# A streamed-weight segment recurrence on one core: other granules stream, and their left passes move along

## The chip, the cores and the metric

The kernel runs on one core of one Trainium2 chip. The metric is the device time of one execution in microseconds. The engines are TensorE (PE, with its weight loads PEld), VectorE (DVE), ScalarE (ACT), GpSimd (POOL) and SyncE (SP), which here does nothing but issue transfers; 16 DMA engines move the data.

## What is computed

The output is the sum of three terms over `x` of 2048 x 1024 in bf16. The first is `x` itself. The second is an attention over 64 segments of 32 rows, in which each segment is preceded by 8 rows of memory, and the first 8 output rows of a segment are the memory of the next one. The third is an expert layer on the two rows with the highest router score. Cut to what matters:

```python
for s in range(n_seg):                      # 64 segments, one after the other
    h = concatenate([mem, xs], axis=1)      # 8 + 32 rows of 1024
    q, k, v = h @ Wq, h @ Wk, h @ Wv        # 32 heads of 128
    p = softmax(mask(q @ k.T * scale))
    o = (p @ v) @ Wo                        # 40 x 4096 @ 4096 x 1024
    mem = o[:, :M, :]                       # goes into the next segment
    outs.append(o[:, M:, :])
...
return x + A(xn) + B(xn)                    # xn: x with its rows normalised
```

The segments form a chain through `mem`, so all four weight matrices (8 MB each in bf16) are used again in each of 64 steps.

## The kernel before

The weights are cut into 64 **granules** of 128 partitions x 2048 columns, 512 KB each. Granules 0 to 47 are six phases of eight: q0, k0, q1, k1, v0, v1 (`PHASES`: matrix and half of the heads); granules 48 to 63 are the output projection. On-chip memory holds 44 of them for the whole run (`resident`, tiles `wres`). The other 20, listed in `STREAMED`, are loaded again in each segment, through a ring of `N_SLOT` = 5 tiles `g` of the pool `wstream`. In segment 0 they come from the inputs; copies of them are made meanwhile in a scratch tensor `wsc`, from which all later segments read. Granule 6 is streamed only in segment 0, since afterwards it stays in PSUM (`KEPT_WHOLE`); of granule 25 half stays there (`KEPT_PART`). So a later segment streams 18 whole granules and a half.

A segment runs through its granules in the order of their numbers. At each it does the **main** matmuls: four of 512 columns into `PSm` for granules 0 to 47 (L817), eight of 256 columns into `WO` for 48 to 63 (`project`, L586). At fixed places (`hook`) the attention work of the segment is put between them. Transfers are issued on SP in program order: when a streamed granule is done with, `release` calls `after`, and that calls `fetch`, which issues the next transfer of the endless list `flow` at L366. This issue waits for the slot's last reader on TensorE, which is the use of the granule five places earlier in the list.

Of a segment's 32 rows, 24 go through the main matmuls beside the 8 memory rows. The other 8 (the **left** rows) do not depend on the memory. They are gathered over four segments (a group) and go through the weights once per group, ahead of their use. That is a **left pass**: four matmuls of 512 columns per granule, into `PSl` (`left_pass`, L579) or `WL` (`project_left`, L598). The table `PASSES` says where each one runs: for a unit (q0, k0, q1, k1, v0, v1, o) and a place (segment of the group, phase, position) the granules whose left pass runs there. Phase 6 is the output projection, places 7 and 8 are the seam between two segments: 7 stands behind the add at L885 (`X <- WO, X`) that makes the new memory, 8 behind the turn of that memory into `ST`, the next segment's operand. A granule that is resident can have its pass anywhere; a streamed one has it where it is used anyway, or is held in its slot until then (`held`). `COPIES` says where a finished unit is copied out of PSUM.

In segment 0, SP issues the loads of residents, of `x` (tiles `XP`) and of the first streamed granules in one list, interleaved by granule number; the tiles `XP`, `MISC` and `XR` lie in the homes of the last residents, which are loaded when the statistics of the rows and the router scores (L254, L256) are done with them. In the last segment each resident's home that comes free takes a granule of the expert weights (`fetch_moe`).

Of the kernel before, what the change touches and what calls it, by code (L numbers as in the profile page):

```python
# [22 lines left out]

PHASES = [(0, 0), (1, 0), (0, 1), (1, 1), (2, 0), (2, 1)]

STREAMED = [2, 5, 6, 9, 13, 17, 21, 25, 29, 33, 36, 39, 42, 45, 47, 50, 53, 56, 59, 62]

UNIT_PHASE = {"q0": 0, "k0": 1, "q1": 2, "k1": 3, "v0": 4, "v1": 5, "o": 6}
PASSES = {
# [11 lines left out]
}  # L44

COPIES = {"q0": (1, 1, 0, "scalar"), "q1": (1, 5, 7, "vector"), "k0": (2, 2, 0, "scalar"), "k1": (2, 5, 7, "vector"),
# [4 lines left out]
def kernel(  # L51
# [44 lines left out]

    streamed = STREAMED
    assert len(streamed) == NG - N_RES
# [915 lines left out]
```

## Time and profile before

| | |
|---|---|
| median of 3 runs | 1866.62 us (1864.03 to 1872.82) |
| profiled execution | 1871.21 us |
| its span | 1869.1 us |
| instructions | 80529 |
| mean granted TensorE clock | 0.957 |
| bytes moved | 712.27 MB, mean 381 GB/s |

A row of the views names line, engine, operation and `out<-in` by the program's tiles. In the waits, "a <- b: t, n, m" says that a stood idle t us in all, n times and at most m us at once, until b. A row of the windows is start:end and length in us, then busy us (and instructions) of TensorE, its weight loads, VectorE, ScalarE and GpSimd, then the granted TensorE clock, the share of the 16 DMA engines' time and GB/s. That share can be a little over 1 since the records of packets overlap. In the order of time a row starts with its start and length in us and merges equal instructions (x8); what stands in brackets is the idle time ahead of it and what ended it.

### The profile page before, as it was taken

The numbers are of one execution on the slowest core, as the hardware profiler recorded it, in microseconds if no ns is written. First come the engines' busy times: TensorE is split into PE (matmuls) and PEld (weight loads), VectorE is DVE, ScalarE is ACT, GpSimd is POOL, SyncE is SP. The second block draws the span as 40 slices with busy tenths as digits, with TensorE's granted clock in tenths as the row PEclk, the third lists the DMA queues.
The fourth block names the chain that finished last, engine by engine and source line by source line (L and its number), as shares of the span: only waits on it lengthen the run. The fifth ranks groups of instructions, "written<-read, shape, count | busy, mean of one in ns | idle before, by whom it ended". The sixth has DMA issues, their size and how long they took to land.

```text
span 1869.1 us, 80529 instructions
## 1 busy us (share of the span) xinstructions
PE 1568.8 (84%) x34978; PEld 847.9 (45%) x34978; DVE 896.9 (48%) x2950; ACT 683.6 (37%) x1933; POOL 457.1 (24%) x898
## 2 busy tenths in 40 slices
PE   3458998898998988888899988988889988988764
PEld 1124444444444444444444444444445544444433
DVE  6725544554455444544554455544544455445430
ACT  1113433444343433434344334434334343433320
POOL 3111322213231322223132322323132221312220
PEclk8669999999999999999999999999999999999995
DMA  9999999999999999999999999999999999999998
GB/s 370 406 355 373 388 386 380 393 382 387 394 385 392 366 383 391 359 380 385 388 375 388 389 384 387 373 396 374 378 369 396 394 382 383 378 377 352 384 402 338
DMA packets 230322, 712.27 MB, mean 381 GB/s; under 512 B 39040, under 2 KB 52912, under 8 KB 229968
## 3 DMA queue, kind: packets, MB, share of 16 engines
q1 hardware_dynamic: 192592, 671.18, 93.0%
q0 software_dynamic: 28736, 28.08, 4.7%
q10 hardware_dynamic: 8640, 7.87, 1.2%
q8 instruction: 274, 4.49, 0.9%
q14 instruction: 80, 0.66, 0.1%
HBM read 694.32 MB, written 22.29 MB: 383 GB/s over the span
## 4 chain that ended last, share of the span: by engine, by line
DMA 61%; PE 32%; DVE 4%; issue 1%; ACT 1%; SPq 0%; ACTq 0%; DVEq 0%
DMA g<-wsc 54%; PE PSm L817 17%; PE WO L586 4%; PE PSl L579 4%; PE BT L649 2%; DMA XP<-in_A_x_dram 2%; PE WL L598 1%; DMA MW<-in_B_w_gate_dram 1%; DVE XR L256 1%; DMA MW<-in_B_w_up_dram 1%; DMA g<-in_A_Wq_dram 1%; DMA wres<-in_A_Wo_dram 1%; DMA g<-in_A_Wo_dram 1%; DMA MW<-in_B_w_down_dram 1%; DMA g<-in_B_w_down_dram 1%
## 5 line engine op out<-in xcount | busy, mean ns | idle before, releaser
L817 PE MATMUL PSm<-wres,ST 128*32 128x512 bf16 x8448 | 700.5, 383 | 6.5 <-DMA wres<-in_A_Wv_dram 3.5
L817 PEld LDWEIGHTS <-ST 128*32 128x32 bf16 x12288 | 323.6, 96 | 412.7 <-issue 168.2
L817 PE MATMUL PSm<-g,ST 128*32 128x512 bf16 x3588 | 360.0, 386 | 97.7 <-DMA g<-wsc 76.3
L586 PEld LDWEIGHTS <-OT 128*32 128x32 bf16 x8192 | 217.6, 97 | 166.6 <-issue 141.0
L836 ACT CAST XB<-PSm 128x512 bf16<-128x512 f32 x256 | 150.7, 589 | 283.9 <-PE PSm L817 280.8
L586 PE MATMUL WO<-wres,OT 128*32 128x256 bf16 x5632 | 237.6, 278 | 12.3 <-DMA wres<-in_A_Wo_dram 8.0
L495 POOL DMA_DIRECT2D LX<-ql_d x63 | 35.4, 562 | 814.0 <-PE WO L586 423.2
L586 PE MATMUL WO<-g,OT 128*32 128x256 bf16 x2560 | 133.3, 281 | 84.1 <-DMA g<-wsc 72.6
L579 PE MATMUL PSl<-wres,STL 128*32 128x512 bf16 x2112 | 184.5, 390 | 0.4 <-issue 0.4
L887 POOL DMA_DIRECT2D out_dram<-X x256 | 130.2, 515 | 211.9 <-DVE X L885 169.4
L664 DVE COPY KT<-BT 128x512 bf16<-128x512 bf16 x112 | 45.9, 410 | 278.7 <-issue 121.8
L281 POOL DMA_DIRECT2D X<-in_A_x_dram x256 | 130.1, 515 | 179.6 <-PE PSm L817 88.8
L389 ACT COPY BK<-KEPT 128x512 bf16<-128x512 bf16 x126 | 74.3, 590 | 131.2 <-PE WO L586 99.8
L657 ACT COPY QT<-BT 128x512 bf16<-128x512 bf16 x128 | 75.0, 586 | 127.1 <-PE BT L502 78.1
L649 PEld LDWEIGHTS <-XB 128*128 128x128 bf16 x1024 | 58.6, 98 | 117.1 <-ACT XB L836 75.2
L885 DVE TENSOR_TENSOR X<-WO,X 128x256 bf16<-128x256 f32 x64 | 27.2, 425 | 172.3 <-PE WO L586 172.3
L649 PE MATMUL BT<-IDENT,XB 128*128 128x128 bf16 x1024 | 102.2, 223 | 8.2 <-ACT XB L836 6.7
L579 PEld LDWEIGHTS <-STL 128*32 128x32 bf16 x3072 | 84.0, 98 | 53.0 <-issue 8.5
L846 ACT CAST VM<-PSm 128x512 bf16<-128x512 f32 x128 | 76.5, 598 | 83.3 <-PE PSm L817 82.8
L736 PEld LDWEIGHTS <-VM 32*128 32x128 bf16 x2048 | 65.1, 91 | 83.7 <-issue 72.7
L393 DVE COPY g<-KEPT 128x512 bf16<-128x512 bf16 x126 | 47.6, 420 | 101.7 <-PE PSm L817 51.5
L681 DVE TENSOR_TENSOR BS<-BS,CT 128x96 f32<-128x96 f32 (+1 forms) x256 | 59.1, 231 | 72.8 <-PE BS L674 68.3
(175 smaller groups left out, 2371.9 us busy)
## 6 DMA issues: line engine op xcount, KB each, us to landing
g<-wsc SPq DMA_DIRECT2D x1134, 512.0 KB, 6.0
g<-wsc SPq DMA_DIRECT2D x63, 256.0 KB, 5.7
LX<-ql_d POOLq DMA_DIRECT2D x63, 128.0 KB, 5.6
ql_d<-XBl ACTq DMA_DIRECT2D x60, 128.0 KB, 5.8
MW<-in_B_w_gate_dram SPq DMA_DIRECT2D x16, 448.0 KB, 9.5
MW<-in_B_w_up_dram SPq DMA_DIRECT2D x16, 448.0 KB, 9.1
wres<-in_A_Wk_dram SPq DMA_DIRECT2D x12, 512.0 KB, 11.9
MW<-in_B_w_down_dram SPq DMA_DIRECT2D x12, 512.0 KB, 10.1
```

What stands on the lines that cost most here:

```text
L281: nc.gpsimd.dma_start(out=X[s % 2][32 * g:32 * g + XM, :], in_=x2[s * SEG:s * SEG + XM, 256 * g:256 * (g + 1)])
L389: copy(out=back[c][:, :], in_=KEPT_COLS[KEPT_WHOLE][c])
L579: nc.tensor.matmul(PSl[32 * jq:32 * jq + 32, :], lhsT=STL[:, g % KC, :], rhs=part(Gv, jq), start=first_, stop=last_, tile_position=(0, 32 ...
L586: nc.tensor.matmul(PS[32 * g:32 * g + 32, 0:256], lhsT=lhs(h), rhs=Gv[:, D * hs + 256 * g:D * hs + 256 * (g + 1)], start=(first and hs == ...
L649: nc.tensor.transpose(out=PTq[:, il, :, :].rearrange("p j r -> p (j r)"), in_=XB[:, il * P:(il + 1) * P], identity=IDENT[:, :])
L657: nc.scalar.copy(out=QT[half][:, :, :], in_=pv)
L681: nc.vector.tensor_tensor(out=S4, in0=S4, in1=m, op=ALU.add)
L736: nc.tensor.matmul(o, lhsT=VM[half][q0:q0 + 32, il * P:(il + 1) * P], rhs=PTm[q0:q0 + 32, il, 0:NK], start=True, stop=False, tile_position ...
L817: nc.tensor.matmul(PSm[32 * jq:32 * jq + 32, :], lhsT=ST[:, kc, :], rhs=part(Gv, jq), start=(kc == 0), stop=(kc == KC - 1), tile_position= ...
L836: nc.scalar.copy(out=XB[:, :], in_=PSm[:, :])
L846: nc.scalar.copy(out=VM[half][:, :], in_=PSm[:, :])
L887: nc.gpsimd.dma_start(out=out2[s * SEG:s * SEG + XM, 256 * g:256 * (g + 1)], in_=OB[32 * g:32 * g + XM, :])
```

## The change

The list of streamed granules changes, and the table of left passes with it, so that each streamed granule still has its left pass at its own place. The number of streamed granules, of passes and of their places at the seam stays.

```diff
-STREAMED = [2, 5, 6, 9, 13, 17, 21, 25, 29, 33, 36, 39, 42, 45, 47, 50, 53, 56, 59, 62]
+STREAMED = [1, 5, 6, 9, 12, 16, 20, 25, 28, 32, 35, 38, 41, 44, 47, 51, 54, 57, 60, 63]
...
-    "o": {(3, 6, 3): [50], (3, 6, 5): [53], (3, 6, 8): [56], (3, 6, 11): [59], (3, 6, 14): [62], (3, 7, 0): [48, 49, 51],
+    "o": {(3, 6, 3): [51], (3, 6, 6): [54], (3, 6, 9): [57], (3, 6, 12): [60], (3, 6, 15): [63], (3, 7, 0): [48, 49, 50],
```

The other lines of the table change in the same way. The pass of granule 50 ran one place behind its use, (3, 6, 3); that of 51 runs at its use. How the order of transfers moves is seen on SP. First, SP from the output stage of one segment over the seam into the next, before (the number behind `wsc` is the granule):

```order
L366 DMA g_2448<-wsc47_118 128x2048
L366 DMA g_2504<-wsc50_119 128x2048
L366 DMA g_2534<-wsc53_120 128x2048
L366 DMA g_2578<-wsc56_121 128x2048
L366 DMA g_2608<-wsc59_122 128x2048
L366 DMA g_2647<-wsc62_123 128x2048
L366 DMA g_2694<-wsc2_105 128x2048
L366 DMA g_2744<-wsc5_106 128x2048
```

and now, where all lines have moved down by one (L366 is L367):

```order
L367 DMA g_2437<-wsc47_118 128x2048
L367 DMA g_2462<-wsc51_119 128x2048
L367 DMA g_2530<-wsc54_120 128x2048
L367 DMA g_2548<-wsc57_121 128x2048
L367 DMA g_2608<-wsc60_122 128x2048
L367 DMA g_2655<-wsc63_123 128x2048
L367 DMA g_2702<-wsc1_105 128x2048
L367 DMA g_2758<-wsc5_106 128x2048
```

Each row stands for the same place in the list; five output granules are one position later, and the first one of the next segment is one earlier, so that the last and the first are now two positions and the seam apart instead of four and the seam.

Second, SP in the middle of a segment, before:

```order
L366 DMA g_2108<-wsc13_108 128x2048
L366 DMA g_2164<-wsc17_109 128x2048
L366 DMA g_2178<-wsc21_110 128x2048
L366 DMA g_2204<-wsc25_111 128x1024
L366 DMA g_2238<-wsc29_112 128x2048
L366 DMA g_2266<-wsc33_113 128x2048
L366 DMA g_2297<-wsc36_114 128x2048
L366 DMA g_2361<-wsc39_115 128x2048
L366 DMA g_2398<-wsc42_116 128x2048
L366 DMA g_2423<-wsc45_117 128x2048
```

and now:

```order
L367 DMA g_2116<-wsc12_108 128x2048
L367 DMA g_2158<-wsc16_109 128x2048
L367 DMA g_2178<-wsc20_110 128x2048
L367 DMA g_2204<-wsc25_111 128x1024
L367 DMA g_2234<-wsc28_112 128x2048
L367 DMA g_2259<-wsc32_113 128x2048
L367 DMA g_2289<-wsc35_114 128x2048
L367 DMA g_2361<-wsc38_115 128x2048
L367 DMA g_2385<-wsc41_116 128x2048
L367 DMA g_2415<-wsc44_117 128x2048
```

All but 25, which is the half granule, are due one position earlier.

Third, SP in segment 0, where the loads of residents (L145), of `x` (L212) and of streamed granules (L364) stand in one list, before:

```order
L212 DMA XP5_317<-in_A_x_dram 128x2x1024
L145 DMA wres15_319<-in_A_Wk_dram 128x2048
L145 DMA wres16_332<-in_A_Wq_dram 128x2048
L364 DMA g_334<-in_A_Wk_dram 128x2048
L212 DMA XP6_347<-in_A_x_dram 128x2x1024
L145 DMA wres18_360<-in_A_Wq_dram 128x2048
L212 DMA XP7_373<-in_A_x_dram 128x2x1024
L145 DMA wres19_375<-in_A_Wq_dram 128x2048
L364 DMA g_377<-in_A_Wq_dram 128x2048
```

and now (L146, L213, L365), from the same row of the list on:

```order
L146 DMA wres15_317<-in_A_Wk_dram 128x2048
L365 DMA g_319<-in_A_Wk_dram 128x2048
L213 DMA XP5_343<-in_A_x_dram 128x2x1024
L146 DMA wres17_345<-in_A_Wq_dram 128x2048
L146 DMA wres18_358<-in_A_Wq_dram 128x2048
L213 DMA XP6_371<-in_A_x_dram 128x2x1024
L146 DMA wres19_373<-in_A_Wq_dram 128x2048
L365 DMA g_375<-in_A_Wq_dram 128x2048
L365 DMA g_428<-in_A_Wq_dram 128x2048
L213 DMA XP7_441<-in_A_x_dram 128x2x1024
```

The last tile of `x`, XP7, stands three rows further down, behind the transfers of granules 19, 16 and 20.

17 rows, old and new, of the table PASSES are left out of this document.

## The prediction

> **What bounds the kernel now.** I read the page first (busy shares, bytes, chain), then the table of waits, then windows cut by segment, then the order of time on TensorE inside one segment.
>
> ```profile
> PE 1568.8 (84%) x34978; PEld 847.9 (45%) x34978; DVE 896.9 (48%) x2950; ACT 683.6 (37%) x1933; POOL 457.1 (24%) x898
> ...
> DMA 61%; PE 32%; DVE 4%; issue 1%; ACT 1%; SPq 0%; ACTq 0%; DVEq 0%
> DMA g<-wsc 54%; PE PSm L817 17%; PE WO L586 4%; PE PSl L579 4%; PE BT L649 2%; DMA XP<-in_A_x_dram 2%; PE WL L598 1%; DMA MW<-in_B_w_gate_dram 1%; DVE XR L256 1%; DMA MW<-in_B_w_up_dram 1%; DMA g<-in_A_Wq_dram 1%; DMA wres<-in_A_Wo_dram 1%; DMA g<-in_A_Wo_dram 1%; DMA MW<-in_B_w_down_dram 1%; DMA g<-in_B_w_down_dram 1%
> ...
> g<-wsc SPq DMA_DIRECT2D x1134, 512.0 KB, 6.0
> g<-wsc SPq DMA_DIRECT2D x63, 256.0 KB, 5.7
> ```
>
> TensorE is busy 84%, yet the chain that ended last lies for 54% in one transfer, the streamed granule g<-wsc. From the two issue rows, 1134 x 0.524 MB + 63 x 0.262 MB = 611 MB, or 9.70 MB in each of 63 segments. How long a segment lasts is read from the add that closes it, and what TensorE waits for from the view of the tile g:
>
> ```profile
> L885 DVE TENSOR_TENSOR X<-WO,X x64: 424/425/427, 129.5 to 1810.4; 128x256 bf16<-128x256 f32 x64
> ...
>   DMA g<-wsc: 149.0, 304
> ```
>
> (1810.4 - 129.5) / 63 = 26.68 us a segment; of these TensorE waits 149.0 / 63 = 2.37 us for streamed granules. Next four successive segments, cut where that add ends, and ahead of them a stretch of the first loading, where transfers are not held back by slots:
>
> ```profile
> 40.00:80.00 40.00, 17.01 (x206) 7.05 (x206) 31.28 (x71) 5.41 (x11) 9.59 (x19) 0.66 1.02 406
> ...
> 1010.30:1036.70 26.40, 23.43 (x540) 12.53 (x536) 12.73 (x41) 10.19 (x30) 4.82 (x10) 1.00 1.00 384
> 1036.70:1063.20 26.50, 24.50 (x560) 13.24 (x556) 12.39 (x43) 10.62 (x31) 7.20 (x14) 1.00 1.02 395
> 1063.20:1089.50 26.30, 23.18 (x523) 12.42 (x518) 13.99 (x50) 11.30 (x33) 10.29 (x19) 1.00 1.02 381
> 1089.50:1116.20 26.70, 23.43 (x540) 12.79 (x536) 12.84 (x41) 10.11 (x30) 4.95 (x10) 1.00 1.01 373
> ```
>
> The last two columns are the share of the DMA engines and GB/s. The engines are taken at 1.00 to 1.02 in every segment, against 1.02 in the loading: there is nearly no idle time in them to win. They move 383 GB/s on average, so 383 x 26.5 = 10.1 MB a segment; at the 406 GB/s of the loading that takes 25.0 us, and TensorE needs 23.2 to 24.5 us. So the transfers set the period. Inside one segment (the one that starts at 1064.0) it looks like this, by windows:
>
> ```profile
> 1064.00:1068.00 4.00, 4.00 (x76) 2.05 (x76) 1.02 (x3) 0.75 (x2) 3.83 (x9) 1.00 0.98 358
> 1068.00:1074.00 6.00, 5.87 (x132) 2.88 (x128) 2.90 (x11) 2.98 (x7) 2.29 (x5) 1.00 1.01 366
> 1074.00:1081.00 7.00, 6.03 (x140) 2.81 (x132) 5.48 (x16) 3.94 (x12) 3.10 (x5) 1.00 1.03 394
> 1081.00:1089.50 8.50, 6.48 (x183) 4.44 (x180) 4.29 (x19) 3.39 (x13) 0.59 (x1) 1.00 1.02 400
> ```
>
> For ten microseconds TensorE is full (4.00 of 4.00, 5.87 of 6.00) and waits for nothing; from granule 33 on it waits (6.48 of 8.50). The waits sit late, where the output projection is.
>
> **How much the ring forgives.** The five slots of g are refilled by the issue at L366; its view says how long a transfer takes.
>
> ```profile
> DMA to landing us min/median/max: 3.3/6.0/10.3
> ```
>
> With 19 transfers in 26.68 us a slot comes round every 5 x 1.40 = 7.0 us, 6.0 of them in flight. The shortest took 3.3 us, so about 2.7 us of the 6.0 are standing in a queue. A slot that comes back up to 2.7 us late still finds the engines busy with the others. The Trainium skill, page "DMA: Bandwidth & Descriptors", section "Anatomy of one DMA — SWDGE (gpsimd) path", gives a transfer about 2.0 us fixed and bytes over 436 GB/s besides; an estimate by that is 3.2 us for 512 KB, close to the 3.3 us here though this stream is issued from another queue. By that estimate the margin would be 2.8 us, and the rule speaks against a gain from any respacing.
>
> **The change, part by part.** Nothing is added or removed in bytes, transfers or matmuls: twenty granules stream as before, and each left pass is run once. Counts of instructions on VectorE, ScalarE and GpSimd stay, in the same order. What moves is where in a segment a streamed granule is due. In time, at the seam between two segments:
>
> ```profile
> 1087.16 0.40 PE L586 MATMUL WO<-g,OT 128*32 128x256 bf16 x8 [0.35 <-DMA g<-wsc]
> 1087.38 0.62 PE L586 MATMUL WO<-wres,OT 128*32 128x256 bf16 x16
> 1088.39 0.40 PE L586 MATMUL WO<-g,OT 128*32 128x256 bf16 x8 [0.39 <-DMA g<-wsc]
> 1088.61 0.40 PE L586 MATMUL WO<-wres,OT 128*32 128x256 bf16 x8
> 1088.82 0.83 PE L579 MATMUL PSl<-wres,STL 128*32 128x512 bf16 x12
> ...
> 1090.25 0.60 PE L817 MATMUL PSm<-wres,ST 128*32 128x512 bf16 x8
> 1090.68 0.39 PE L817 MATMUL PSm<-g,ST 128*32 128x512 bf16 x4
> ```
>
> These are granules 59, 60 and 61, 62 (with a wait of 0.39 us), 63, the left passes of the seam, 0 and 1, and 2. One granule's main matmuls take 0.22 us of TensorE in either form (1088.39 to 1088.61; 1090.25 to 1090.68 for two).
>
> 1. Output stage: 50, 53, 56, 59, 62 become 51, 54, 57, 60, 63, each due one position, 0.22 us, later. Were the transfers to land when they do now, the wait there would fall by 0.22 us a segment, once and not five times, since a wait at 51 also delays 54: at most 63 x 0.22 = -14 us.
> 2. Earlier stages: 2, 13, 17, 21, 29, 33, 36, 39, 42, 45 become 1, 12, 16, 20, 28, 32, 35, 38, 41, 44, each due 0.22 us earlier: at most +14 us, by the same count. In the segment shown nothing waits up to granule 29, so part of this is covered there, but only as long as the transfers don't slip. The value I take for 1 and 2 together is 0: over a whole segment 18.5 granules still need the engines for the same time, and a wait taken from the output stage comes back at 35, 38, 41 and 44, which are now four granules at three positions each. Ends: -14 and +14.
> 3. The seam. From 62 to 2 pass 2.29 us (1088.39 to 1090.68), so the refill after it is 0.89 us later than the even 1.40; with 63 and 1 it is 1.86 us (1088.61 to 1090.47). The queue of 2.7 us covers both. The rate is low around the seam (358 GB/s with the engines at 0.98), but GpSimd is busy there 3.83 of 4.00 us with its small transfers. Were the 0.04 between 0.98 and 1.02 all due to the hole, over 4 us and halved, it were 0.08 us a segment, -5 us. I take 0; ends 0 and -5.
> 4. A new hole. In the fourth segment of each group 44 and 47 stand on both sides of the left passes of v1; in time, with 45 and 47 as streamed granules:
>
> ```profile
> 1052.31 0.40 PE L817 MATMUL PSm<-wres,ST 128*32 128x512 bf16 x4
> ...
> 1053.16 0.40 PE L817 MATMUL PSm<-g,ST 128*32 128x512 bf16 x4
> ...
> 1054.66 0.40 PE L817 MATMUL PSm<-g,ST 128*32 128x512 bf16 x4
> ```
>
> These are 44, 45 and 47. The distance becomes 2.35 us (44 to 47) instead of 1.50, in 16 segments: 16 x 0.85 = +14 us if nothing stands in the queue, 0 with 2.7 us in it. I take 0, nearest to the queue that was measured.
> 5. Moved issues in the first segment. XP7, the last tile of x, is issued three transfers later on SP, so at 0.524 MB over 406 GB/s 3 x 1.29 = 3.9 us later; the statistics of all rows wait for it, and after them TensorE, VectorE's 16 router tiles and the homes that these give back. What speaks for no cost:
>
> ```profile
> PE PSm L817 <- DMA g<-in_A_Wq_dram: 11.2, 1, 11.2
> ...
> PE WO L586 <- DMA wres<-in_A_Wo_dram: 8.0, 4, 6.3
> ...
> PE WO L586 <- DMA g<-in_A_Wo_dram: 6.1, 3, 2.7
> ```
>
> TensorE waits 11.2 us for a transfer at granule 17 already, and 14.1 us again for the last weights of that segment: being 4 us late in between is hidden by those 14.1 us. Ends 0 and +4; I take 0.
> 6. The last segment and the expert part: as many residents lie ahead of granule 47 as before, and the expert weights start behind the same fetch: 0.
>
> Sum: 0 us. Against the profiled execution that is 1871.21 (span 1869.1 and 2.1 around it); it lies 4.6 over the median of 1866.62. On the median the forecast is 1867.
>
> A rule of the Trainium skill bears on the limit: "DMA: Bandwidth & Descriptors", section "Where 436 GB/s comes from", lets 358 GB/s bind for transfers from HBM and 435 for the fabric. The trace disagrees with 358, as segments run at 373 to 395 and the loading at 406. By 358 nothing could be won; by 435, an estimate from 10.1 MB is 23.3 us a segment, and spacing would decide up to TensorE's own 24.5.
>
> **Rivals.**
> - *The relief stays, the price is covered* (faster): granules 12 to 32 are due while TensorE is full and nothing waits, so they come free 0.22 us earlier and the engines get their work earlier too. That is -14 us, 1853. For it: no wait before 33 in the segment shown, and engines at 0.98 to 1.01 there against 1.03 later. Against it: a lead of 0.22 us is small beside a queue of 2.7 us.
> - *The output stage gives nothing, the three-position run is paid* (slower): 32 to 44 are taken faster than they land, the wait moves there whole, and the longer distances behind it (44 to 47, 47 to 51) let the queue run empty. It costs +14 us, 1881, and decides from the point at which fewer than two transfers are queued when 44 is used. For it: the engines reach 1.03 and 394 GB/s in that stage, with TensorE waiting already. Against it: the median of 6.0 us.
> - *The order isn't changed as said*: the rows of SP's order show that it is; no chance of its own.
>
> **How the numbers follow.** Forecast 0.50, its own range 1860 to 1874 (the runs of before spread from 1864 to 1873); faster rival 0.28 at 1853; slower rival 0.22 at 1881. The range of 8 in 10 takes in both rivals' centres and leaves out what lies beyond: 1852 to 1881. Half a per cent, 9.3 us, is about what a measurement of this kernel can tell from no change: faster by more than that 0.28, within it 0.50, slower 0.22.
>
> **What would show it.** Right: the wait of TensorE for g<-wsc stays near 149 us in all, with less of it at L586 and more at L817, and a segment stays at 26.6 to 26.7 us. The faster rival shows as a sum well under 149 with the engines nearer 1.02; the slower one as more wait at L817 without less at L586. Step 5 is wrong if the first L885 comes after 131 us. All of it is wrong if the distance between segments changes with the bytes and the engines' share as they are.

## The result and the profile after

| | before | after |
|---|---|---|
| median of 13 runs each, on one chip | 1865.73 us (1858.56 to 1872.88) | 1880.82 us (1870.83 to 1886.65) |
| profiled execution | 1871.21 us | 1880.82 us |
| its span | 1869.1 us | 1878.8 us |

The changed kernel takes 1.0082 times as long (95% interval 1.0061 to 1.0102): slower by some 15 us, where no change was forecast. The spans of the profiled pair show 9.7 us of it, as the profiled execution of before lies 5.5 us over its median. Single executions of one kernel spread by 10 to 30 us, so totals are read from the ratios below, and the profiles, one execution each, are read for where time stands.

First the page of the changed kernel: busy engines, bytes, instruction packets, and the chain that ended last. All line numbers are one higher than before (L817 is L818, L586 is L587, L885 is L886).

```profile
PE 1574.2 (84%) x34978; PEld 842.3 (45%) x34978; DVE 896.6 (48%) x2950; ACT 685.4 (36%) x1933; POOL 457.2 (24%) x898
...
DMA packets 230323, 712.27 MB, mean 379 GB/s; under 512 B 39040, under 2 KB 52912, under 8 KB 229968
...
q8 instruction: 274, 4.49, 0.9%
...
DMA 57%; PE 33%; DVE 4%; issue 3%; ACT 1%; POOL 1%; SPq 0%; ACTq 0%; DVEq 0%; POOLq 0%
```

The bytes and the number of matmuls are the same. The rate fell from 381 to 379 GB/s. In the chain the transfers lost four points (61% to 57%), and "issue", time in which an engine waits for nothing that the profile shows, gained two (1% to 3%). The same is seen in the waits of TensorE and in the view of the tile g:

```profile
PE PSm L818 <- DMA g<-wsc: 102.3, 188, 2.0
PE WO L587 <- DMA g<-wsc: 25.6, 60, 1.1
PE WO L587 <- issue: 21.3, 27, 1.7
...
PE PSl L580 <- issue: 4.3, 6, 1.8
```

```profile
  DMA g<-wsc: 128.0, 248
```

against these of before:

```profile
PE PSm L817 <- DMA g<-wsc: 76.3, 154, 2.5
PE WO L586 <- DMA g<-wsc: 72.6, 150, 2.0
...
PE WO L586 <- issue: 5.5, 7, 1.1
```

In the output projection the wait for streamed granules fell by 47.0 us (72.6 to 25.6). Of these, 26.0 came back at the granules ahead of it (76.3 to 102.3), so that TensorE waits 21 us less for streamed granules in all: the view of the tile g, the single row above, has 128.0 us, 248 times, where it had 149.0, 304 times. And yet the segments are longer, by the add that closes them:

```profile
L886 DVE TENSOR_TENSOR X<-WO,X x64: 423/425/426, 131.2 to 1819.5; 128x256 bf16<-128x256 f32 x64
```

(1819.5 - 131.2) / 63 = 26.80 us instead of 26.68, or 7.4 us over 63 segments; 1.7 us more stand ahead of the first add, and the last 0.6 behind the last. Four successive segments, cut at that add, with the engines' share and GB/s at the end of each row, show the transfers as full as before:

```profile
1043.10:1069.00 25.90, 24.22 (x559) 13.50 (x559) 12.58 (x43) 10.75 (x31) 7.20 (x14) 1.00 1.01 385
1069.00:1096.30 27.30, 23.27 (x527) 12.31 (x518) 13.92 (x50) 11.41 (x33) 10.34 (x19) 1.00 1.01 380
1096.30:1122.40 26.10, 23.74 (x540) 12.85 (x536) 12.74 (x41) 10.15 (x30) 4.95 (x10) 1.00 1.01 382
1122.40:1150.00 27.60, 23.76 (x540) 12.62 (x536) 12.70 (x41) 10.20 (x30) 4.82 (x10) 1.00 1.00 376
```

Following TensorE's order through the trace, each wait for a granule can be put to the granule's position. The table has the waits between the first 63 of those adds, divided by 62, in us a segment. It counts the waits under 0.15 us too, which the views leave out, so that it has 2.52 where the view's 149.0 us are 2.37 over 63 segments. The last column is read from the rows of the closing add, as above:

| kernel | granules 1-21 | 24-34 | 35-47 | 50-63 | all granules | "issue" | segment |
|---|---|---|---|---|---|---|---|
| before | 0.49 | 0.07 | 0.75 | 1.22 | 2.52 | 0.16 | 26.68 |
| after | 0.84 | 0.06 | 0.80 | 0.43 | 2.13 | 0.56 | 26.80 |
| output granules alone (e1) | 0.53 | 0.07 | 0.60 | 0.78 | 1.99 | 0.37 | 26.53 |
| second half alone (f2) | 0.59 | 0.10 | 0.96 | 0.68 | 2.33 | 0.34 | 26.74 |
| half bytes, old positions (h1) | 0.01 | 0.00 | 0.00 | 0.80 | 0.80 | 0.28 | 25.16 |
| half bytes, second half moved (h2) | 0.00 | 0.00 | 0.01 | 0.45 | 0.46 | 0.29 | 24.54 |
| 30, 34, 37 and the new output granules (h3) | 0.55 | 0.00 | 0.65 | 0.93 | 2.14 | 0.29 | 26.65 |

So 0.79 us a segment left the output stage. It came back as 0.35 at granules 1 to 21, which are those of the next segment, and as 0.40 of "issue"; at 35 to 47 only 0.05 appeared. These sums balance (2.52 + 0.16 before, 2.13 + 0.56 after), and all idle time of TensorE between these adds is 3.02 us a segment in both. The 0.12 us by which a segment is longer stand in TensorE's busy time (23.66 and 23.78; on the page, 1568.8 and 1574.2 us for the same 34978 matmuls). Busy time hides waits, as two rows of before show:

```profile
1067.92 0.39 PE L817 MATMUL PSm<-g,ST 128*32 128x512 bf16 x4
1068.13 0.60 PE L817 MATMUL PSm<-wres,ST 128*32 128x512 bf16 x8
```

Four matmuls of 512 columns start together and show 0.38 us each (the profile models the ends of matmuls), but the next four start 0.21 us after them. A start up to 0.17 us late leaves no idle time. An estimate from start to start, each step compared with the lower quarter of the equal steps of before, has 21.5 us of TensorE's own work in a segment of either kernel. It puts 3.74 us of lateness at streamed granules before and 3.31 after: 1.77 and 0.76 in the output stage, 1.08 and 1.27 at 35 to 47, 0.77 and 1.19 at 1 to 21. Lateness for nothing visible goes from 0.43 to 0.93. Counted so, too, the granules alone cost less than before in this pair of executions, and what the profile shows nothing for turns the sum.

### The profile page after: what moved, and what is told of

Same layout as the page of the kernel before. It is cut to its first block, busy times and chain, and to the rows that moved or that the text cites. A ratio compares the mean times of both kernels' runs of the same rounds, so it can differ in the third digit from the quotient of the medians.

```text
span 1878.8 us, 80544 instructions
## 1 busy us (share of the span) xinstructions
PE 1574.2 (84%) x34978; PEld 842.3 (45%) x34978; DVE 896.6 (48%) x2950; ACT 685.4 (36%) x1933; POOL 457.2 (24%) x898
## 4 chain that ended last, share of the span: by engine, by line
DMA 57%; PE 33%; DVE 4%; issue 3%; ACT 1%; POOL 1%; SPq 0%; ACTq 0%; DVEq 0%; POOLq 0%
DMA g<-wsc 49%; PE PSm L818 15%; PE WO L587 6%; PE PSl L580 4%; PE BT L650 2%; PE WL L599 2%; DMA g<-in_A_Wk_dram 1%; DMA MW<-in_B_w_gate_dram 1%; DMA XP<-in_A_x_dram 1%; DVE XR L257 1%; DMA MW<-in_B_w_up_dram 1%; DMA wres<-in_A_Wo_dram 1%; PE WO L737 1%; PE BS L737 1%; PE BT L302 1%
## 5 line engine op out<-in xcount | busy, mean ns | idle before, releaser
L818 PE MATMUL PSm<-wres,ST 128*32 128x512 bf16 x8448 | 662.9, 384 | 1.8 <-DVE ST L325 1.4
L818 PEld LDWEIGHTS <-ST 128*32 128x32 bf16 x12288 | 324.2, 96 | 472.9 <-issue 183.5
L818 PE MATMUL PSm<-g,ST 128*32 128x512 bf16 x3588 | 360.1, 388 | 117.7 <-DMA g<-wsc 102.3
L587 PE MATMUL WO<-wres,OT 128*32 128x256 bf16 x5632 | 247.8, 278 | 32.1 <-issue 16.7
L587 PEld LDWEIGHTS <-OT 128*32 128x32 bf16 x8192 | 211.8, 97 | 134.2 <-issue 112.8
L587 PE MATMUL WO<-g,OT 128*32 128x256 bf16 x2560 | 132.8, 278 | 36.1 <-DMA g<-wsc 25.6
L650 PEld LDWEIGHTS <-XB 128*128 128x128 bf16 x1024 | 58.7, 98 | 110.0 <-issue 54.8
L886 DVE TENSOR_TENSOR X<-WO,X 128x256 bf16<-128x256 f32 x64 | 27.2, 425 | 150.2 <-PE WO L587 150.2
L663 ACT COPY KT<-QKL 128x128 bf16<-128x128 bf16 x128 | 38.2, 298 | 153.0 <-PE BT L650 153.0
## 6 DMA issues: line engine op xcount, KB each, us to landing
LX<-ql_d POOLq DMA_DIRECT2D x63, 128.0 KB, 5.4
ql_d<-XBl ACTq DMA_DIRECT2D x60, 128.0 KB, 5.7
```

What stands on the lines that cost most here:

```text
L587: nc.tensor.matmul(PS[32 * g:32 * g + 32, 0:256], lhsT=lhs(h), rhs=Gv[:, D * hs + 256 * g:D * hs + 256 * (g + 1)], start=(first and hs == ...
L650: nc.tensor.transpose(out=PTq[:, il, :, :].rearrange("p j r -> p (j r)"), in_=XB[:, il * P:(il + 1) * P], identity=IDENT[:, :])
L818: nc.tensor.matmul(PSm[32 * jq:32 * jq + 32, :], lhsT=ST[:, kc, :], rhs=part(Gv, jq), start=(kc == 0), stop=(kc == KC - 1), tile_position= ...
```

## The experiments

Each ratio is to the kernel before, run on the same chip, with its 95% interval. "Second half" means 28, 32, 35, 38, 41, 44; "first half" 1, 12, 16, 20. The left passes are moved along with the granules in each kernel, as in the change.

### Which granules cost

**Output granules alone (e1).**

```diff
-... 42, 45, 47, 50, 53, 56, 59, 62]
+... 42, 45, 47, 51, 54, 57, 60, 63]
```

> Only the output granules move (51, 54, 57, 60, 63; the rest as before). Theory A, TensorE's own instruction fetch is the new wait of the output stage: its waits for g<-wsc at L586 fall from 72.6 us to about 30, its waits put down to issue rise from 10 us to 25 to 35, and the ratio to before is 1.002 to 1.009. Theory B, the run of three-position steps 32 to 44 costs the time: this kernel is at 0.993 to 1.000, with issue waits near 10 us.

Measured 0.9987 (0.9963 to 1.0011): no difference that can be told. That is the range of theory B; A wanted at least 1.002. In its profile L586 waits 47.1 us for g<-wsc instead of 72.6, and nothing of it comes back at L817; 8.5 us come back as "issue" there (5.5 to 14.0), and 22 us of "issue" stand in all stages together instead of 9.5:

```profile
PE PSm L817 <- DMA g<-wsc: 71.8, 155, 1.8
PE WO L586 <- DMA g<-wsc: 47.1, 100, 1.1
PE WO L586 <- issue: 14.0, 20, 1.6
```

**All but the output granules (e2).**

```diff
-STREAMED = [2, 5, 6, 9, 13, 17, 21, 25, 29, 33, 36, 39, 42, 45, 47, ...
+STREAMED = [1, 5, 6, 9, 12, 16, 20, 25, 28, 32, 35, 38, 41, 44, 47, ...
```

> Only the earlier granules move (1, 12, 16, 20, 28, 32, 35, 38, 41, 44; the output granules as before). Theory A: issue waits stay near 10 us, and the ratio is 0.998 to 1.004. Theory B: the wait at L817 rises from 76.3 us to 100 or more, and the ratio is 1.006 to 1.010.

Measured 1.0067 (1.0042 to 1.0092), as theory B has it. The loss is here: being due earlier costs, and being due later gains nothing that can be told. In this profile, too, the granule waits are fewer in sum (137.8 us) and "issue" is more (29 us in all):

```profile
PE PSm L818 <- DMA g<-wsc: 101.8, 190, 2.5
PE WO L587 <- DMA g<-wsc: 36.0, 77, 1.4
PE WO L587 <- issue: 15.3, 19, 1.7
```

Next this part was cut in two.

**First half alone (f1)**, and **second half alone (f2).**

```diff
-STREAMED = [2, 5, 6, 9, 13, 17, 21, 25, 29, ...
+STREAMED = [1, 5, 6, 9, 12, 16, 20, 25, 29, ...
```

> The old list with 1, 12, 16, 20 alone moved (2, 13, 17, 21 before). Theory B1, the run 28 to 44 of the changed list costs the 0.7 per cent: this kernel is at 0.997 to 1.002. Theory B2, the cost comes from the early granules (the seam and the first segment): 1.004 to 1.008, with the first closing add at 131.5 us or later.

```diff
-... 25, 29, 33, 36, 39, 42, 45, 47, ...
+... 25, 28, 32, 35, 38, 41, 44, 47, ...
```

> The old list with 28, 32, 35, 38, 41, 44 alone moved (29, 33, 36, 39, 42, 45 before). Theory B1: 1.004 to 1.008, with the waits for g<-wsc gathered at 35 to 44 and the fourth segment of a group at 26.4 us or more. Theory B2: 0.997 to 1.002, first closing add at 130 us.

First half 1.0015 (0.9985 to 1.0044), second half 1.0069 (1.0037 to 1.0101). The second half alone costs about what all of it costs, and its waits show what it does:

```profile
PE PSm L818 <- DMA g<-wsc: 100.4, 185, 2.3
PE WO L587 <- DMA g<-wsc: 39.8, 84, 1.6
```

It takes 32.8 us off the output stage (72.6 to 39.8), though no output granule moved, and puts 24.1 us on L818 (76.3 to 100.4). In the trace, the transfer of granule 50 is issued 6.21 us ahead of the first matmul of granule 48, on average over the segments, instead of 5.53.

**The change without the second half (g1)**, the counter-test, and **28, 32, 35, 38 alone (g2).**

```diff
+STREAMED = [1, 5, 6, 9, 12, 16, 20, 25, 29, 33, 36, 39, 42, 45, 47, 51, 54, 57, 60, 63]
```

> The whole change but for 28 to 44, which stay at 29, 33, 36, 39, 42, 45. If the parts add up (0.9987 for the output granules, 1.0015 for the first half): 0.998 to 1.003, and 28 to 44 carry the loss of the whole change. If the loss is one of the parts together: 1.005 or more.

```diff
-... 25, 29, 33, 36, 39, 42, 45, 47, ...
+... 25, 28, 32, 35, 38, 42, 45, 47, ...
```

> The old list with 28, 32, 35, 38 moved, and 42 and 45 left. If 41 and 44, around the left passes of v1, carry the loss of 0.7 per cent: 0.998 to 1.002. If 35 and 38 carry it: 1.005 to 1.008. Shared: 1.003 to 1.005.

g1 1.0030 (1.0002 to 1.0059), g2 1.0038 (1.0013 to 1.0062). Without the second half most of the 0.8% is gone; what is left in g1 is about the first half's 0.15% and what can't be told from it. In the second half the loss seems shared between 28 to 38 and the pair 41, 44, but the 0.31% between g2 and f2 has an error of 0.4%.

### The hole around the left passes of v1

**The change with 42 and 45 at their old positions (f3).**

```diff
-... 35, 38, 41, 44, 47, 51, ...
+... 35, 38, 42, 45, 47, 51, ...
```

> The changed list with 42 and 45 back in place of 41 and 44, so that the hole between 44 and 47 around the left passes of v1 is gone. Theory H, that hole lets the queue run dry: the fourth segment of a group falls from 26.42 to about 26.2 us, its DMA share rises, and the ratio to before is 1.000 to 1.005 against the 1.008 of the whole change. Without it: 1.007 to 1.010.

Measured 1.0045 (1.0018 to 1.0072): some of the loss goes, but that takes out both the hole and two early granules. The fourth segments of a group, which theory H saw falling to about 26.2 us, stay at 26.40 in its trace. To part the two, the left passes of v1 on residents were left out, five of eight. With the positions of the second half, three of these five stand between 44 and 47: from the one to the other TensorE takes 1.89 us in g4's fourth segments, instead of 2.35, and 1.70 in its other segments. The base (g3) and the second half (g4) both have this edit.

```diff
+        if u == "v1" and g not in streamed:
+            return
```

> The kernel before with the left passes of v1 on resident granules left out (five of eight, 1.1 us of TensorE in each fourth segment; that part of the computation is left out). Theory H, the fourth segment is TensorE's there while the ring is full: 0.989 to 0.996, since up to 1.1 us x 16 go. If the transfers set that segment too: 0.997 to 1.001.

> The old list with 28 to 44 moved, and the same five left passes of v1 left out. Theory H: the loss against the old list in the same form shrinks from 0.7 to under 0.3 per cent, since the wait ahead of the passes is made good behind them. If the loss is one of the waits at 35 to 44 in every segment: still 0.5 to 0.8 per cent.

g3 0.9944 (0.9918 to 0.9970), g4 1.0039 (1.0010 to 1.0067). g4 / g3 = 1.0096, with an error of about 0.004 from the two intervals: the second half costs as much without the passes as with them. The hole is not the cause. g3 itself came out in the range of theory H: taking about 1.1 us of TensorE's work out of every fourth segment, 17.6 us in sum, won some 10 us. So TensorE's own work counts there beside the transfers.

### The late tile of x

**The change with XP7 at its old row in segment 0 (f4).**

```diff
+            if g == 1:
+                load_x(n_x)
+                n_x += 1
```

> The changed kernel with the tiles of x issued as early as before in segment 0 (XP7 in the row that it had). If the late x costs: the first closing add is at 130 us instead of 131.6, and the ratio to before falls from 1.008 by 0.001 to 0.002. If it is hidden: 131.6 us as it was.

Measured 1.0072 (1.0038 to 1.0107), which the ratio can't tell from the change's own 1.0082. The first closing add shows the step by itself:

```profile
L889 DVE TENSOR_TENSOR X<-WO,X x64: 424/425/427, 129.1 to 1821.2; 128x256 bf16<-128x256 f32 x64
```

129.1 us, as early as before (129.5), against 131.2 in the change. In the change XP7 is issued at 34.8 us instead of 30.5 and lands at 53.7 instead of 45.3, 8.4 us later. The first closing add of one kernel against another varies by a microsecond or two, but the five profiles with the late tile (after, e2, f1, f3, g1) have it at 129.8 to 131.6, and the nine with the early one, with all bytes and the projection as it was, at 128.0 to 130.0. The late tile costs about 2 us once.

### Waits for nothing that the profile shows

"Issue" at L587 grew from 5.5 to 21.3 us. In the order of time of TensorE one of these waits looks like this:

```profile
1092.53 0.39 PE L587 MATMUL WO<-g,OT 128*32 128x256 bf16 x8
1092.75 0.28 PE L587 MATMUL WO<-wres,OT 128*32 128x256 bf16 x3
1094.33 0.61 PE L587 MATMUL WO<-wres,OT 128*32 128x256 bf16 x13 [1.31 <-issue]
```

It breaks a run of equal matmuls on a resident tile: no operand is awaited. The records of single packets hold one of 16 KB on the instruction queue (q8) that started at 1092.01 and took 0.92 us; the matmul started 1.40 us after it had landed. All 46 such waits (of 0.15 us or more) of the changed kernel between 150 and 1805 us, 34.5 us in sum, and all 15 of before, 9.5 us, follow such a packet by 1.2 to 1.6 us and stand at the same place modulo 256 in the count of TensorE's instructions. TensorE runs 70136 instructions, weight loads counted, which is 274 x 256 but for 8, and 274 such packets were sent: 16 KB for 256 instructions make 64 bytes each. So these are, by all signs of the trace, waits for TensorE's own instructions.

To see what they are worth, the output projection was written with half as many matmuls, each twice as wide, in the change (**e3**) and in the kernel before (**e4**). The sums of the two heads are not added there, which leaves that part of the computation out.

```diff
-            for g in range(4):
-                nc.tensor.matmul(PS[32 * g:32 * g + 32, 0:256], lhsT=lhs(h),
...
+            for c in range(2):
+                r0 = 64 * hs + 32 * c
+                nc.tensor.matmul(PS[r0:r0 + 32, :], lhsT=lhs(h), rhs=Gv[:, D * hs + 512 * c:D * hs + 512 * (c + 1)],
...
```

> The changed kernel with the output projection of the main rows as four matmuls of 512 columns per granule in place of eight of 256: the same columns through TensorE with half the instructions there; the two heads' sums lie in different rows and are not added, which leaves that part of the computation out. Theory A: issue waits fall from 34 us to under 8, and the time is at 0.990 to 1.000 of before, level with or under the old list in the same form. Theory B: still 0.6 to 1.0 per cent over the old list in the same form.

> The kernel before with the output projection as four matmuls of 512 columns (the two heads' sums not added, as above). Theory A: little to win, since issue waits are 10 us before: ratio 0.993 to 1.000. Theory B: the same; the two theories differ in how the new list in this form stands to this one.

e3 1.0009 (0.9983 to 1.0035), e4 0.9958 (0.9932 to 0.9985). All the waits of TensorE that these two profiles put to g<-wsc or to issue, first e3:

```profile
PE PSm L818 <- DMA g<-wsc: 112.9, 223, 2.0
...
PE WO L588 <- DMA g<-wsc: 42.8, 89, 1.5
...
PE GU L961 <- issue: 7.3, 3, 2.6
```

then e4:

```profile
PE WO L587 <- DMA g<-wsc: 79.3, 162, 1.8
PE PSm L817 <- DMA g<-wsc: 76.8, 153, 1.7
...
PE GU L960 <- issue: 7.2, 3, 2.6
...
PE BS L674 <- issue: 0.2, 1, 0.2
```

The waits for instructions are gone (what is left at GU is in the expert part, and is there in every kernel). And now the wait for granules only moves: 79.3 to 42.8 in the output stage, 76.8 to 112.9 before it, in sum 156.1 and 155.7. Yet e3 stays above e4 by 1.0009 / 0.9958 = 1.0051, with an error of about 0.0037. Theory A has them level, B has 0.6 to 1.0%, and this lies between. What went with the instruction waits, 0.3 of the 0.8%, has an error of about 0.4%. Of the 0.5% that stays, the late tile holds part: the first closing add is at 134.1 us in e3 and at 131.0 in e4, 0.17% of the time. The other 0.34% is within its error, so that this pair doesn't show a loss that has neither the instruction waits nor the late tile in it. Nor do the instruction waits alone go with the loss: e1 has 22 us of them and loses nothing, f2 has 20 us and loses 0.69%.

### Are the transfers the cause, or TensorE's own order

**Half the bytes for the streamed granules below 48, with the old positions (h1) and with the second half moved (h2).**

```diff
-        return slice(0, 1024 if s > 0 and g == KEPT_PART else 2048)
+        return slice(0, 1024 if s > 0 and g < 48 else 2048)
...
+                if s > 0 and g in streamed and g not in KEPT_COLS:
+                    Gv = [Gv[:, 0:512], Gv[:, 512:1024]] * 2
```

> The kernel before, with only the first 1024 columns of the streamed granules of the phases 0 to 47 loaded from segment 1 on; the matmuls take those twice, so half of these weights is left out of the computation. It is the base for the next kernel. 12 granules of 0.524 MB become 0.262 MB, so a segment moves 3.1 MB less of some 10.1 MB, and transfers need 17.3 us at 406 GB/s; TensorE becomes the bound. Each theory expects 24.5 to 25.5 us a segment, ratio 0.92 to 0.95 to the kernel before, and a wait for g<-wsc under 40 us in all.

> The second half moved (28, 32, 35, 38, 41, 44), with the same halved transfers. Theory T (the second half costs what transfers that are due earlier cost): with the transfers off the path its ratio is that of the kernel with halved bytes and the old positions, within 0.2%. Rival F (the moved passes cost TensorE time of themselves, by order of matmuls, tails that are not seen as waits, or its instruction fetch): it stays 0.5% or more above it, as the second half does with whole transfers (1.0069).

h1 0.9414 (0.9384 to 0.9444), h2 0.9256 (0.9220 to 0.9292). The first is in the range expected, with 48.2 us of waits instead of under 40; 13 whole granules were halved, not the 12 of the expectation. The second is as neither theory had it: the second half moved is 0.983 of the old positions, with an error of about 0.005, a gain of 1.7% where it loses 0.7% with all bytes. The waits of h1 and h2:

```profile
PE WO L586 <- DMA g<-wsc: 47.7, 87, 2.1
...
PE WO L586 <- issue: 13.6, 16, 1.7
...
PE PSm L819 <- DMA g<-wsc: 0.5, 1, 0.5
```

```profile
PE WO L587 <- DMA g<-wsc: 27.5, 48, 2.3
...
PE WO L587 <- issue: 10.3, 15, 1.4
...
PE PSm L820 <- DMA g<-wsc: 0.3, 1, 0.3
```

How busy the engines are is seen from windows over the same stretch, h1 and h2:

```profile
200.00:1700.00 1500.00, 1382.28 (x31878) 758.75 (x31867) 767.55 (x2589) 625.27 (x1787) 405.33 (x791) 0.99 0.84 270
```

```profile
200.00:1700.00 1500.00, 1382.97 (x32377) 771.26 (x32370) 774.07 (x2617) 631.89 (x1799) 408.13 (x796) 0.99 0.86 280
```

With the engines at 0.84 and 0.86 of their time, nearly all waits for granules are those of the output stage: five whole ones, three positions apart, ask for 0.524 MB in 3 x 0.22 = 0.66 us, 790 GB/s, nearly twice the 406 of the loading. A use that comes earlier in the second half frees its slot earlier, and the output granules are fetched earlier (granule 50 is issued 5.84 us ahead of the first matmul of 48 in h2, 5.03 in h1), so that L587 waits 20 us less. Nothing comes back ahead of it, where the engines have room, and the instruction waits don't grow (0.28 and 0.29 us a segment). So the moved passes cost TensorE nothing of themselves, and F falls. The same relief exists with all bytes (72.6 to 39.8 in f2); that it ends as a loss there goes with the full transfer stream.

**The opposite direction: 30, 34, 37 in place of 29, 33, 36, with the new output granules (h3) and alone (h4).**

```diff
-... 25, 29, 33, 36, 39, 42, 45, 47, ...
+... 25, 30, 34, 37, 39, 42, 45, 47, ...
```

> The output granules of the changed kernel (51, 54, 57, 60, 63), and 30, 34, 37 in place of 29, 33, 36, one position later than before. Theory T: what is due later in the second half gains as what is due earlier costs (28, 32, 35, 38 cost 0.38%): ratio 0.994 to 0.998. Rival A (the old positions of the second half are at the optimum, each shift costs): 1.001 or more.

> Only 30, 34, 37 in place of 29, 33, 36, all else as before. Theory T: 0.995 to 0.999, and the wait at 35 to 47 falls. Rival A: 1.001 or more.

h4 0.9994 (0.9972 to 1.0017) decides nothing, since its interval takes in the upper end of T's range (0.999), no change, and rival A's 1.001. In its profile the wait at 35 to 47 is 0.58 us a segment instead of 0.75, as T has it. h3 0.9970 (0.9944 to 0.9996) is inside T's range and below 1 by little, the one version with all of the computation whose interval lies below 1. From e1's 0.9987 it can't be told apart.

## Why the prediction was wrong

The median of 1880.82 lies just inside the stated range of 1852 to 1881, but only since that range reached out to the slower rival. The forecast itself, no change with a chance of 0.50, failed, and it failed in steps 1 and 2.

- **The bound** was read rightly in the main: halving the bytes below granule 48 takes 6% off, so the transfers set the period, though not alone, as g3 shows. A segment of h2, with 0.46 us of granule waits left, takes 24.54 us, at the upper end of the 23.2 to 24.5 that was read from four segments. Those were busy times, which have hidden waits in them. The Trainium skill, page "DMA: Bandwidth & Descriptors", section "Where 436 GB/s comes from", has HBM transfers bound at 358 GB/s, the rate of an HBM stack divided between two cores. The changed kernel's segments above, on the one core that runs here, move 376 to 385, so that rule again isn't what holds them.
- **Steps 1 and 2 failed**, in "the value I take for 1 and 2 together is 0 ... a wait taken from the output stage comes back at 35, 38, 41 and 44". Four parts of it were off. The one segment that was shown has no wait up to granule 29, but on average 0.49 us a segment stood at granules 1 to 21 already, so that being due earlier was less covered there than it looked. The relief in the output stage was taken for 0.22 us a segment at most; it was 0.79, since the earlier second half also has the output granules fetched sooner (f2: 32.8 us less wait, with no output granule moved). It hardly came back at 35 to 47 (+0.05 a segment) but at granules 1 to 21 of the next segment (+0.35) and as waits for instructions (+0.40). And the two did not cancel: the earlier granules cost 0.67% (e2, of which about 0.1 is the late tile's), the later ones gave back nothing that can be told (e1).
- **The slower rival** named the price (+14 us, 1881; the median is 1880.82) and the place (32 to 44), and f2 puts the loss there. That the price is met so closely is in part luck: about 2 of the 15 us are the late tile's, which it didn't contain, and its mechanism was only half right. "The output stage gives nothing" is false, as that stage gave 47 us. That the wait moves ahead of it is right for f2 (+24.1 us at L818). Whether it decides "from the point at which fewer than two transfers are queued" wasn't measured.
- **Step 3** (seam): 0 was taken. e1, where 63 is followed by 2, shows no difference; g1, where 63 is followed by 1, is at 1.0030 with the late tile in it. Granules 1 to 21 do wait longer in the change, 0.84 against 0.49, but only 0.53 in e1. A price of the seam alone isn't shown.
- **Step 4** (new hole) was right at 0: with the hole cut from 2.35 to 1.89 us the second half costs the same (g4 / g3).
- **Step 5** (XP7 later) was taken at 0, with an end of +4, and was to be wrong if the first closing add came after 131 us. It came at 131.2, and f4 has it back at 129.1: about 2 us. XP7 landed 8.4 us later, not 3.9, and the later waits for weights didn't hide all of it.
- **Step 6**: the time from the last closing add to the end of the span is 59.3 us against 58.7 (1878.8 - 1819.5 and 1869.1 - 1810.4): 0 was right to 0.6 us.
- **What would show it**: less wait at L586 and more at L817 came true, but the sum fell to 128.0 instead of staying near 149, and a segment has 26.80 instead of 26.6 to 26.7. The last sign, that all of it is wrong if the distance between segments changes with the bytes and the engines' share as they are, is what came. The view that the forecast leaned on, the wait for g<-wsc, went down by 21 us while the kernel became slower. It wasn't the measure of the loss: "issue" at TensorE, 9.5 us before, grew by 25, and part of each wait stands in the busy time.

What stays open: how the 0.8% is divided. The longer first segment, about 2 us, holds 0.1%. The waits for instructions hold 0.3% by e3 against e4, with an error of 0.4%. The rest goes with the full transfer stream (h1 against h2), but by which step an equal number of bytes takes longer isn't shown: the engines' share reads 1.00 to 1.01 in each of the four segments above, and the rate differs by half a per cent, no more than single executions differ.

## What to carry to other kernels

When a stream is bound by its transfers, a wait that shrinks in one stage, or in the sum, proves nothing. Add up all the waits of the engine, those for nothing visible too, remember that overlapping instructions hide short ones, and judge by the period. Here being due earlier cost time with the transfers full, and gained when they weren't: the same edit gave +0.7% and -1.7%. A slot ring ties a stage to the one before it, so a burst at the end (here five granules, three positions apart) was relieved by what is used earlier, and the price has to be looked for there and in the next round.

## What the chip showed beyond that

- **TensorE waits for its own instructions.** They come in packets of 16 KB on queue q8, one for each 256 instructions, 274 packets of nearly 1 us each, one in about 6.4 us. The waits are 9.5 us before and 34.5 after, and they appear where waits for granules go; that a packet lands unnoticed while a granule is awaited fits this, but isn't shown by itself. Full engines are not needed for it: with these at 0.84, h1 has 18 us of such waits ahead of the expert part. They fall on stages of short matmuls (27 of the 46 at L587, where a matmul has 256 columns). With half the instructions there (242 packets in the run), they are gone.
- **A busy engine can be late.** Groups of matmuls that show 0.38 us and start 0.21 us apart hide up to 0.17 us of each wait; the estimate from start to start has 3.74 us a segment where the idle time has 2.52.
- **A mean rate hides a burst**: at 280 GB/s over the span, far below the 406 of the loading, h1 still waits 47.7 us for the output granules.
